# A two-part block on one core: other queues and engines for the first loads, and PSUM tiles by column part at the end

## The chip, the core and the metric

The kernel runs on one core of a Trainium2 chip. A core has TensorE (matmul, with its weight loads), VectorE, ScalarE, GpSimd and SyncE, each with its own instruction stream; the matmul sums go to PSUM, everything else lives in SBUF, and transfers between SBUF and the chip's main memory are issued by an engine's queue (here SyncE's, called SP below, and ScalarE's) and carried out by 16 DMA engines. The metric is the device time of one execution in microseconds (us). Before the change it is 1164.75 us, the median of three runs from 1164.68 to 1164.84.

## What is computed

All in float32, for 2048 tokens of 576 numbers:

```python
x = A_x
xn = _layernorm(x, axis=-1)
return x + _A_ref(xn, A_wqkv, A_wo) + _B_ref(xn, B_w1, B_w2)
```

`_A_ref` is an attention of 32 heads of 18 numbers over a dilated window: each token looks at itself and at the seven tokens 2, 4, ... 14 places before it; the result goes through `wo`. `_B_ref` is a two-layer network with a hidden width of 4608, `relu(xn @ w1) @ w2`. Both take the same normalised input and are added to `x`.

## The kernel before

**Precision.** TensorE multiplies in a faster format with fewer bits (float32r). Each operand is therefore split into a high part, the value rounded to that format, and a low part, the rest; a product takes three matmul terms (high by high, high by low, low by high). `two` (lines 144 to 150) splits a loaded weight: ScalarE copies the high part, then VectorE, or GpSimd for the steps in `by_pool`, subtracts it from the source. The normalised tokens are split in the same way when they come out of the transpose (`transpose_split`, lines 276 to 308): ScalarE writes the high part of `xT`, VectorE the low part.

**Tiling.** The tokens are dealt to two phases (`ph`) of eight tiles (`i`) of 128 tokens; pairs of tiles make four blocks of 256 tokens (`tb`). The hidden width is cut into 36 strips of 128, in 12 groups of three (`c`, `f`). One slot is one (phase, group, block, strip): `h_mm` makes 14 matmuls of 256 columns into a `ph` tile in PSUM, ScalarE and VectorE write the relu's high and low parts, and two slots later `o_mm` multiplies them by `w2`. `o_mm` handles the block's two token tiles `k` = 0 and 1, and cuts the 576 output columns in two parts `CUT`, 0 to 256 and 256 to 576, since one matmul's result must lie in one PSUM bank. Both parts of a `k` share one tile `po` of the pool `ps_o`, which has two such tiles of two banks; `half` (line 572) picks the part. After three strips `o_out` adds the sum to the accumulator, which is the tile of `x` itself. 288 slots make the whole; the attention's work is put between them by the tables `todo` and `todo_late`, and the order of all instructions is written out (`manual_schedule`).

**The opening** (lines 680 to 757) is written by hand. Line 102 sets TensorE to 24 transposes of the identity. Then the code issues the loads of `x` 0 and `x` 1 (each in two column halves, one on SP's queue and one on ScalarE's, lines 233 to 237), an Exp of one spare column on ScalarE, whose table is loaded ahead of it, the first strip of `w1`, `x` 2, three more weight strips, `x` 3, and so on. A strip of `w1` is a staging tile `st` of 640 columns: 512 rows of `w1` as four column groups, and the last 64 rows twice, in the upper and the lower partitions of the fifth (lines 157 to 162), three transfers on SP. The statistics of `x` 0 (`stats`: `bn_stats` by VectorE for each half, `bn_aggr`, an addition, two small operations by GpSimd) are followed by its normalisation on ScalarE (lines 269 and 270); those of `x` 1 by its normalisation on VectorE (line 272). TensorE transposes both (lines 286 and 287). For `x` 0 the four full groups go to one tile of `ps_m` and the rest to another; for `x` 1 both go to one tile of `ps_o`. `run_splits(-9)` on line 695 stands between the transposes of `x` 0 and its high part: it is the split of the first `w1` strip, whose step is `HEADW[0]`, -9. The first real matmuls (line 701) need its high part and the high parts of both token tiles.

**The end.** The last slot (`end` in `o_mm`) sorts its matmuls so that within each `k` the part 256 to 576 comes first, then the part 0 to 256. `o_out` (lines 611 to 617) then adds, for `k` = 0 and 1, part 1 and part 0, and issues each part's output behind its add: part 1 on ScalarE's queue, part 0 on SP's, but the very last part in two halves of 64 partitions, one on each queue. For all earlier groups one add of 576 columns (line 606) is followed, in the last group of a phase, by `done` (line 527), which issues the whole tile's output on SP when it has been called twice for the tile. `left` counts these calls.

Of the kernel before, what the change touches and what calls it, by code (L numbers as in the profile page):

```python
# [10 lines left out]
F32 = mybir.dt.float32  # L11
F32R = mybir.dt.float32r
AF = mybir.ActivationFunctionType
# [4 lines left out]
P = 128  # L18
NPH = 2
NI = 8  # L20
# [5 lines left out]
C = 3  # L26
# [12 lines left out]
HEADW = (-9, -8, -7, -6, -5, -4)  # L39
# [16 lines left out]
def tile_body(ctx: ExitStack, tc: tile.TileContext, x, wqkv, wo, w1, w2, out):  # L56
    nc = tc.nc
    S, D = x.shape
# [5 lines left out]
    KT = 4  # L64
    DR = D - KT * P
    D2 = D // 2
    CUT = (slice(0, 256), slice(256, D))
# [22 lines left out]
    ps_o = pool("ps_o", 2, space=PSUM)  # L90
    ps_h = pool("ps_h", 2, space=PSUM)
    ps_m = pool("ps_m", 2, space=PSUM)
# [10 lines left out]
    for _ in range(WARM):  # L103
        nc.tensor.transpose(warm[:, 0, 0:P], ident, ident)

    x_v = x.rearrange("(p i two) d -> two i p d", i=NI, two=NPH)
    o_v = out.rearrange("(p i two) d -> two i p d", i=NI, two=NPH)


    t = {"pe": 0.0, "dve": 0.0}  # L110

    def mm(o, l, r, start, stop, n):
        nc.tensor.matmul(o, l, r, start=start, stop=stop)  # L113
        t["pe"] += n / 2400.0 + 0.002

    def dve(n):
        t["dve"] += (n + 130) / 960.0
# [6 lines left out]
    def split_task(step, load, split):  # L124
        tasks.append((step, load, split))

    def stage_more(ahead=AHEAD):
        while tasks and len(staged) < ahead:
            step, load, split = tasks.popleft()
            st = stp.tile([P, 640], F32, name="st")  # L130
            load(st)
            staged.append((step, split, st))
# [9 lines left out]
    step_now = None  # L142

    def two(hi, lo, src, n):
        nc.scalar.activation(hi, src, AF.Copy)  # L145
        if step_now in by_pool:
            nc.gpsimd.tensor_tensor(lo, src, f32(hi), op=ALU.subtract)
        else:
            nc.vector.tensor_tensor(lo, src, f32(hi), op=ALU.subtract)  # L149
            dve(n)  # L150
# [3 lines left out]
    def w1_task(step, key, f):  # L154
        def load(st):
            c = slice(f * P, (f + 1) * P)
            nc.sync.dma_start(
                st[:, 0:512].rearrange("p (k c) -> p k c", k=KT),
                w1[0 : KT * P, c].rearrange("(k p) c -> p k c", p=P),
            )  # L160
            nc.sync.dma_start(st[0:DR, 512:640], w1[KT * P : D, c])
            nc.sync.dma_start(st[DR:P, 512:640], w1[KT * P : D, c])

        def split(st):
            w = w1p.tile([P, 2, 5 * P], F32R, name="w1t")
            two(w[:, 0, :], w[:, 1, :], st[:, :], 640)
            W1[key] = w

        split_task(step, load, split)
# [59 lines left out]
    X, XT, XN, MR = {}, {}, {}, {}  # L229

    def load_x(ph, i):
        X[ph, i] = xp.tile([P, D], F32, name="x")
        if ph == 0 and i < 2:
            for h, q in enumerate((nc.sync, nc.scalar)):
                c = slice(h * D2, (h + 1) * D2)
                q.dma_start(X[ph, i][:, c], x_v[ph, i][:, c])
            return
        nc.sync.dma_start(X[ph, i], x_v[ph, i])

    def stats(ph, i, parts=False, act=False):  # L240
        xt = X[ph, i]
# [283 lines left out]
    left = {(ph, i): 2 for ph in range(NPH) for i in range(NI)}  # L525

    def done(ph, i):
        left[ph, i] -= 1
        if left[ph, i] == 0:
            nc.sync.dma_start(o_v[ph, i], X[ph, i])  # L530


    slots = [(ph, c, tb, f) for ph in range(NPH) for c in range(NCH) for tb in range(NTB) for f in range(C)]
    H, PO = {}, {}
# [35 lines left out]
        h_out(n)  # L570

    def half(po, h):
        return po[:, 1, 0 : D - 256] if h else po[:, 0, 256:512]

    def o_mm(n, out=True, which=range(2)):
        ph, c, tb, f = slots[n]
        hi, lo = H[n]
        w = W2[ph, c, f]
        end = n == len(slots) - 1
        for k in which:  # L580
            if f == 0:
                PO[k] = ps_o.tile([P, 2, 512], F32, name="po")
            cs = slice(k * P, (k + 1) * P)
            terms = [(j, l, b, h) for j, (l, b) in enumerate(((hi, 0), (hi, 1), (lo, 0))) for h in range(2)]
            if end:
                terms.sort(key=lambda z: -z[3])
            for j, l, b, h in terms:
                mm(
                    half(PO[k], h), l[:, cs], w[:, b, CUT[h]],
                    f == 0 and j == 0, f == C - 1 and j == 2, D2,  # L590
                )
        if 1 in which:
            H.pop(n)
        if out:
            o_out(n, which)

    def o_out(n, which=range(2)):
        ph, c, tb, f = slots[n]
        if f < C - 1:
            return  # L600
        for k in which:
            i = 2 * tb + k
            acc = X[ph, i]
            if n < len(slots) - 1:
                whole = PO[k].rearrange("p b c -> p (b c)")[:, 256 : 256 + D]
                nc.vector.tensor_tensor(acc, whole, acc, op=ALU.add)  # L606
                dve(D)
                if c == NCH - 1:
                    done(ph, i)
                continue  # L610
            for h, c in reversed(list(enumerate(CUT))):
                nc.vector.tensor_tensor(acc[:, c], half(PO[k], h), acc[:, c], op=ALU.add)  # L612
                if h == 0 and i == NI - 1:
                    for q, p in (nc.sync, slice(0, P // 2)), (nc.scalar, slice(P // 2, P)):
                        q.dma_start(o_v[ph, i][p, c], acc[p, c])
                else:
                    (nc.scalar if h else nc.sync).dma_start(o_v[ph, i][:, c], acc[:, c])
            left[ph, i] -= 1
            assert left[ph, i] == 0


    todo = {}
# [10 lines left out]
    for ph in range(NPH):  # L633
# [22 lines left out]
        if ph + 1 < NPH:  # L656
            e = b + SPP - SPC
            for i in range(NI):
                if i >= len(XT_STEPS):
                    z = e + 3 + 2 * i  # L660
                    at(z - 6, load_x, ph + 1, i)
                    late(z - 2, stats, ph + 1, i)
                    late(z - 1, norm, ph + 1, i)
                    at(z + 1, make_xt, ph + 1, i)
                    continue
                load, first, second, send, back, parts = (e + k for k in XT_STEPS[i])
                at(load, load_x, ph + 1, i)
                late(first, stats, ph + 1, i, False, True)
                late(second, norm_turned, ph + 1, i)
                late(send, xt_a, ph + 1, i)  # L670
                at(back, xt_f, ph + 1, i)
                at(parts, xt_s, ph + 1, i)
# [7 lines left out]
    by_pool.update((-9, -8, *range(UNIT0 - 5, UNIT0)))  # L680
    both, x_low, w_low, last = TERMS[0:4], TERMS[4:8], TERMS[9:13], [TERMS[8], TERMS[13]]
    load_x(0, 0)
    load_x(0, 1)
    nc.scalar.activation(spare, mhalf, AF.Exp)
    stage_more(1)
    load_x(0, 2)
    stage_more(4)
    load_x(0, 3)
# [40 lines left out]
    x2[1]()  # L729
    x2[3]()  # L730
    o_mm(0)
    o_mm(1)
    make_xt(0, 3, bank=ps_h)
    o_mm(2, out=False)
    stats(0, 4)
    s5 = stats(0, 5, parts=True)
# [6 lines left out]
    h4[0]()  # L743
    h4[1]()
    o_out(2, (0,))
    x4 = make_xt(0, 4, parts=True)
    for f in x4[:3]:
        f()
    norm(0, 5)
    o_out(2, (1,))  # L750
    x4[3]()
    h_terms(5, TERMS)
# [51 lines left out]
```

## Time and profile before

| | us |
|---|---|
| median of three runs | 1164.75 (1164.68 to 1164.84) |
| the profiled execution, its own time | 1165.02 |
| its span in the profile | 1163.2 |
| TensorE matmul busy in the span | 1155.8 (99%) |
| VectorE busy | 822.1 (71%) |
| ScalarE busy | 308.7 (27%) |
| GpSimd busy | 44.8 (4%) |

The span is the part of the execution that the profiler's records cover. Times in the rows below are counted from its start. In a row of the timeline stand the start, the length, the engine, the line of the kernel, the operation, output and inputs by the program's names with their shapes (partitions by columns), and how many instructions were merged; what ended an idle time before it stands in brackets. PE is TensorE, DVE VectorE, ACT ScalarE, POOL GpSimd, and SPq and ACTq are the queues of SyncE and ScalarE while they issue transfers. A row of the waits has the engine and what it waited for, then the total in us, how often, and the longest. A row of DMA issues has the transfer, the queue, how often and its size, and the median us from issue to landing. A row of windows has a stretch of time and its length, the busy time and the number of instructions of the five engines (PE, weight loads, DVE, ACT, POOL), the clock granted to TensorE, the busy share of the DMA engines and the GB/s that they moved.

### The profile page before, as it was taken

To read this page: it belongs to the slowest core of one execution; us is meant where nothing else is said; L and a number is where in the kernel's file an instruction comes from. 1 tells how busy PE (TensorE), PEld (TensorE's weight loads), DVE (VectorE), ACT (ScalarE), POOL (GpSimd) and SP (SyncE) were. 2 spreads that over 40 slices of the span, in tenths; PEclk is the share of its full clock that TensorE was granted. 3 is DMA by queue.
4 is the path that set the end of the run, shared out by engine and by line. 5 is a ranking of instruction groups with operands and counts; after the bars stand their busy time and mean duration, and the time that the engine had idled before them with its cause. 6 is when DMAs were issued, how large, how long until landed. Compare 5 with 4: busy or idle time off the path is not lost.

```text
span 1163.2 us, 21702 instructions
## 1 busy us (share of the span) xinstructions
PE 1155.8 (99%) x8916; PEld 1147.9 (99%) x8916; DVE 822.1 (71%) x1299; ACT 308.7 (27%) x748; POOL 44.8 (4%) x60
## 2 busy tenths in 40 slices
PE   8999999999999999999999999999999999999998
PEld 8999999999999999999999999999999999999998
DVE  7427885887687688876683288768768877887843
ACT  5312222131231221322433123222222312222310
POOL 3200100010000000000010001000100000000000
PEclk9999999999999999999999999999999999999999
DMA  5312211140331311364752113031312303113541
GB/s 184 98 34 77 70 47 54 39 112 1 94 81 30 89 34 44 96 163 106 184 159 70 42 53 96 21 81 40 85 36 59 110 1 101 50 31 91 125 99 62
DMA packets 150036, 88.66 MB, mean 76 GB/s; under 512 B 58560, under 2 KB 133824, under 8 KB 149936
## 3 DMA queue, kind: packets, MB, share of 16 engines
q1 hardware_dynamic: 146752, 78.38, 25.1%
q10 hardware_dynamic: 3184, 8.88, 2.6%
q8 instruction: 70, 1.15, 0.4%
q14 instruction: 30, 0.25, 0.1%
HBM read 67.90 MB, written 11.14 MB: 68 GB/s over the span
## 4 chain that ended last, share of the span: by engine, by line
PE 99%; DMA 0%; ACT 0%; DVE 0%; issue 0%; DVEq 0%; POOL 0%; ACTq 0%
PE ph L113 39%; PE po L113 39%; PE pm L113 20%; PE pm L286 0%; DMA x<-in_x 0%; DVE x L612 0%; PE pm L287 0%; DVE bst L250 0%; ACT xn L269 0%; ACT xn L270 0%; ACT xT L291 0%; PE po L286 0%; DVEq L800 0%; PE ph L287 0%; POOL nm L256 0%
## 5 line engine op out<-in xcount | busy, mean ns | idle before, releaser
L113 PE MATMUL ph<-xT,w1t 128*128 128x256 f32 x4018 | 505.1, 277 | 0.7 <-ACT xT L291 0.7
L113 PEld LDWEIGHTS ph<-xT,w1t 128*128 128x128 f32 x4018 | 487.0, 188 | 1.3 <-ACT xT L291 1.0
L113 PE MATMUL po<-w2t,hhi 128*128 128x256 f32 (+1 forms) x2304 | 395.3, 293 | 0.0
L113 PEld LDWEIGHTS po<-w2t,hhi 128*128 128x128 f32 x2304 | 337.3, 188 | 1.1
L556 ACT ACTIVATE hhi<-ph 128x256 fp32r<-128x256 f32 x287 | 109.9, 383 | 582.9 <-PE ph L113 570.5
L113 PE MATMUL po<-w2t,hlo 128*128 128x256 f32 (+1 forms) x1152 | 243.9, 292 | 0.0
L559 DVE SCALAR_TENSOR_TENSOR hlo<-ph,hhi 128x256 fp32r<-128x256 f32 x287 | 120.7, 421 | 165.0 <-ACT hhi L556 164.4
L113 PEld LDWEIGHTS po<-w2t,hlo 128*128 128x128 f32 x1152 | 190.1, 187 | 0.0
L113 PE MATMUL pm<-wq,xT 128*128 128x432 f32 x896 | 185.5, 358 | 0.0
L606 DVE TENSOR_TENSOR x<-po,x 128x576 f32<-128x576 f32 x190 | 143.0, 756 | 60.1 <-PE po L113 57.3
L113 PEld LDWEIGHTS pm<-wq,xT 128*128 128x128 f32 x896 | 163.8, 188 | 5.6
L421 DVE TENSOR_TENSOR pr<-qo,k 128x1152 f32<-128x1152 f32 x64 | 86.1, 1348 | 0.0
L424 DVE TENSOR_REDUCE lg<-pr 128x64 f32<-128x1152 f32 x64 | 85.1, 1343 | 0.0
L451 DVE TENSOR_TENSOR pr<-lg,v 128x1152 f32<-128x1152 f32 x64 | 84.7, 1349 | 0.0
L149 DVE TENSOR_TENSOR w2t<-st,w2t 128x576 fp32r<-128x576 f32 x72 | 55.8, 775 | 31.4 <-ACT w2t L145 31.4
L149 DVE TENSOR_TENSOR w1t<-st,w1t 128x640 fp32r<-128x640 f32 x70 | 58.8, 840 | 20.6 <-ACT w1t L145 20.5
L458 DVE TENSOR_TENSOR pr<-pr 128x288 f32<-128x288 f32 (+1 forms) x128 | 70.5, 600 | 0.0
L145 ACT ACTIVATE w2t<-st 128x576 fp32r<-128x576 f32 x72 | 49.3, 685 | 44.0 <-PE po L113 34.5
L390 ACT ACTIVATE k<-pm 128x144 f32<-128x144 f32 x64 | 18.7, 292 | 146.2 <-PE pm L113 146.2
L145 ACT ACTIVATE w1t<-st 128x640 fp32r<-128x640 f32 x72 | 52.8, 734 | 12.7 <-DMA st<-in_w 6.7
L427 POOL TENSOR_SCALAR_AFFINE_SELECT lg<-lg 1x512 f32<-1x512 f32 x8 | 9.9, 1232 | 810.0 <-DVE lg L424 810.0
L522 DVE TENSOR_TENSOR x<-pm,x 128x256 f32<-128x256 f32 (+1 forms) x32 | 13.1, 453 | 30.8 <-PE pm L113 30.8
(79 smaller groups left out, 461.8 us busy)
## 6 DMA issues: line engine op xcount, KB each, us to landing
st<-in_w SPq DMA_DIRECT2D x72, 288.0 KB, 3.2
st<-in_w SPq DMA_DIRECT2D x72, 256.0 KB, 3.2
st<-in_wqkv SPq DMA_DIRECT2D x32, 216.0 KB, 3.0
turned<-tr SPq DMA_DIRECT2D x64, 80.0 KB, 2.8
xn<-turned SPq DMA_DIRECT2D x16, 320.0 KB, 3.2
st<-in_w SPq DMA_DIRECT2D x144, 32.0 KB, 2.8
x<-in_x SPq DMA_DIRECT2D x14, 288.0 KB, 4.1
out<-x SPq DMA_DIRECT2D x14, 288.0 KB, 2.1
```

Source lines behind the costliest of these rows:

```text
L113: nc.tensor.matmul(o, l, r, start=start, stop=stop)
L145: nc.scalar.activation(hi, src, AF.Copy)
L149: nc.vector.tensor_tensor(lo, src, f32(hi), op=ALU.subtract)
L390: nc.scalar.activation(k[:, W - 1 + i, :], pq[:, 1, :], AF.Copy)
L421: nc.vector.tensor_tensor(pr[i], q, window(k, i), op=ALU.mult)
L424: nc.vector.tensor_reduce(lg[:, i], pr.pop(i).rearrange(heads, d=Dh), axis=AX.X, op=ALU.add)
L451: nc.vector.tensor_tensor(pr[i].rearrange(heads, d=Dh), e, window(v, i).rearrange(heads, d=Dh), op=ALU.mult)
L458: nc.vector.tensor_tensor(o, z[:, 0:n], z[:, n : 2 * n], op=ALU.add)
L522: nc.vector.tensor_tensor(acc, po[h], acc, op=ALU.add)
L556: nc.scalar.activation(hi, pt, AF.Relu)
L559: nc.vector.scalar_tensor_tensor(lo, pt, 0.0, f32(hi), op0=ALU.max, op1=ALU.subtract)
L606: nc.vector.tensor_tensor(acc, whole, acc, op=ALU.add)
```

## The change

There are three edits.

- **The first loads.** Both halves of `x` 0 go on SP's queue. `x` 1 is one transfer of all its columns on ScalarE's queue. It is issued from within the load of the first `w1` strip, whose two 64-row transfers also go on ScalarE's queue, one ahead of `x` 1 and one behind it. `stage_more(1)` therefore moves ahead of the spare Exp.
- **The first high part.** For the step `HEADW[0]`, which is the first `w1` strip alone, VectorE copies the high part.
- **The last two token tiles.** In the last group of three slots, `k` = 0 takes both tiles of `ps_o`, one for each part of the columns, and `k` = 1 takes two tiles of `ps_m`. `x` 6 of the second phase goes out whole by `done` after both adds; the two parts of `x` 7 go out by one transfer each.

```diff
     def two(hi, lo, src, n):
-        nc.scalar.activation(hi, src, AF.Copy)
+        if step_now == HEADW[0]:
+            nc.vector.tensor_copy(hi, src)
+        else:
+            nc.scalar.activation(hi, src, AF.Copy)
...
+            if key == (0, 0, 0):
+                nc.scalar.dma_start(st[0:DR, 512:640], w1[KT * P : D, c])
+                load_x(0, 1)
+                nc.scalar.dma_start(st[DR:P, 512:640], w1[KT * P : D, c])
+                return
             nc.sync.dma_start(st[0:DR, 512:640], w1[KT * P : D, c])
             nc.sync.dma_start(st[DR:P, 512:640], w1[KT * P : D, c])
...
     def load_x(ph, i):
         X[ph, i] = xp.tile([P, D], F32, name="x")
-        if ph == 0 and i < 2:
-            for h, q in enumerate((nc.sync, nc.scalar)):
-                c = slice(h * D2, (h + 1) * D2)
-                q.dma_start(X[ph, i][:, c], x_v[ph, i][:, c])
+        if ph == i == 0:
+            for c in slice(0, D2), slice(D2, D):
+                nc.sync.dma_start(X[ph, i][:, c], x_v[ph, i][:, c])
             return
-        nc.sync.dma_start(X[ph, i], x_v[ph, i])
+        (nc.scalar if (ph, i) == (0, 1) else nc.sync).dma_start(X[ph, i], x_v[ph, i])
...
     def half(po, h):
+        if isinstance(po, list):
+            return po[h]
         return po[:, 1, 0 : D - 256] if h else po[:, 0, 256:512]
...
-            if f == 0:
+            if f == 0 and n == len(slots) - C:
+                if k:
+                    PO[k] = [ps_m.tile([P, c.stop - c.start], F32, name="pm") for c in CUT]
+                else:
+                    PO[k] = [ps_o.tile([P, 2, 512], F32, name="po")[:, 0, 0 : c.stop - c.start] for c in CUT]
+            elif f == 0:
                 PO[k] = ps_o.tile([P, 2, 512], F32, name="po")
...
             for h, c in reversed(list(enumerate(CUT))):
                 nc.vector.tensor_tensor(acc[:, c], half(PO[k], h), acc[:, c], op=ALU.add)
-                if h == 0 and i == NI - 1:
-                    for q, p in (nc.sync, slice(0, P // 2)), (nc.scalar, slice(P // 2, P)):
-                        q.dma_start(o_v[ph, i][p, c], acc[p, c])
-                else:
+                if k:
                     (nc.scalar if h else nc.sync).dma_start(o_v[ph, i][:, c], acc[:, c])
-            left[ph, i] -= 1
-            assert left[ph, i] == 0
+            if k == 0:
+                done(ph, i)
...
     load_x(0, 0)
-    load_x(0, 1)
+    stage_more(1)
     nc.scalar.activation(spare, mhalf, AF.Exp)
-    stage_more(1)
     load_x(0, 2)
```

## The prediction

> **What bounds the kernel now.** I read the head of the page first, then the waits of TensorE over the whole span, then the chain of work that ended last in the opening, and at last the timeline, the DMA issues and the windows at the two places that the change touches.
>
> ```profile
> span 1163.2 us, 21702 instructions
> ...
> PE 1155.8 (99%) x8916; PEld 1147.9 (99%) x8916; DVE 822.1 (71%) x1299; ACT 308.7 (27%) x748; POOL 44.8 (4%) x60
> ```
>
> ```profile
> PE po L104 <- POOL mhalf L99: 1.4, 1, 1.4
> PE pm L286 <- ACT xn L270: 1.2, 1, 1.2
> PE ph L113 <- ACT xT L291: 0.7, 1, 0.7
> ```
>
> These three are all the waits that the profile lists for TensorE: 3.3 us, all in the first 8.84 us. Span less busy is 1163.2 - 1155.8 = 7.4 us; the other 4.1 us lie behind the last matmul. From 8.84 us to that matmul TensorE never waits for anything, so a change in the opening moves everything behind it by the same amount, and a change at the end counts by itself. No part of the change alters the number of matmuls or the order between. Whatever it is worth lies in the first 9 and the last 5 us.
>
> The opening, from the chain of waits (start, length, what):
>
> ```profile
> 0.73 2.92 DMA x<-in_x
> ...
> 3.67 0.83 DVE bst L250 x2
> ...
> 5.08 0.79 ACT xn L269
> ...
> 6.78 0.66 PE pm L286 x4
> ...
> 8.19 0.61 ACT xT L291
> ...
> 8.84 3.74 PE ph L113 x28
> ```
>
> The path to the first real matmul begins with the landing of the first half of x 0 at 3.65 us; statistics (L250, two halves, ending 4.50), normalisation on ScalarE, transposes on TensorE and the copy of x 1's transposes to xT follow with gaps of hundredths. Anything that delays the statistics of x 0 delays the whole kernel.
>
> The end, from the timeline:
>
> ```profile
> 1157.57 0.31 PE L113 MATMUL po<-w2t,hlo 128*128 128x320 f32 x1
> ...
> 1157.95 0.28 PE L113 MATMUL po<-w2t,hlo 128*128 128x256 f32 x1
> ...
> 1158.27 1.60 DVE L612 TENSOR_TENSOR x<-po,x 128x320 f32<-128x320 f32 x4 [3.07 <-PE po L113]
> 1158.36 0.31 PE L113 MATMUL po<-w2t,hlo 128*128 128x320 f32 x1
> ...
> 1158.74 0.28 PE L113 MATMUL po<-w2t,hlo 128*128 128x256 f32 x1
> 1158.80 1.13 ACTq L617 DMA_DIRECT2D out<-x  x2
> ...
> 1159.90 0.52 SPq L615 DMA_DIRECT2D out<-x  x1
> 1160.02 0.55 ACTq L615 DMA_DIRECT2D out<-x  x1
> ```
>
> The sums of the four parts are complete at 1157.88 (x 6, 320 columns), 1158.23 (x 6, 256), 1158.67 (x 7, 320) and 1159.02 (x 7, 256). VectorE begins its first add at 1158.27, 0.04 behind the second of these, though that add needs the first alone. From there the four adds run back to back, to 1159.87. So VectorE is late by 1158.27 - 1157.92 = 0.35 us, and this delay reaches the last output transfer.
>
> **The change part by part: the opening.**
>
> ```profile
> 0.73 0.90 ACTq L236 DMA_DIRECT2D x<-in_x  x2
> 0.73 0.87 SPq L236 DMA_DIRECT2D x<-in_x  x2
> ...
> 1.66 1.28 ACT L684 ACT_TABLE_LOAD   x1 [1.66 <-PEq L786]
> 2.12 0.56 SPq L161 DMA_DIRECT2D st<-in_w  x1
> ...
> 4.84 0.81 DVE L250 BATCH_NORM_STATS2 bst<-x 128x6 f32<-128x288 f32 x2
> ...
> 6.63 0.72 ACT L145 ACTIVATE w1t<-st 128x640 fp32r<-128x640 f32 x1
> 6.75 0.58 DVE L272 TENSOR_SCALAR xn<-x,mv,rstd 128x576 f32<-128x576 f32 x1 [0.67 <-POOL rstd L257]
> ...
> 7.27 0.27 PE L287 MATMUL pm<-ident,xn 128*64 128x128 f32 x1
> ...
> 7.43 1.55 POOL L147 TENSOR_TENSOR w1t<-st,w1t 128x640 fp32r<-128x640 f32 x1 [0.72 <-ACT w1t L145]
> 7.47 0.60 ACT L291 ACTIVATE xT<-pm 128x512 fp32r<-128x512 f32 x1
> ...
> 7.88 0.27 PE L287 MATMUL po<-ident,xn 128*64 128x128 f32 x1
> ...
> 8.10 0.69 DVE L294 TENSOR_TENSOR xT<-pm,xT 128x512 fp32r<-128x512 f32 x1 [0.77 <-ACT xT L291]
> ```
>
> Median microseconds from issue to landing, from the DMA issues of narrow windows (the first two issued at 0.73, the third at about 1.15, the w1 transfer at 1.65):
>
> ```profile
> x<-in_x ACTq DMA_DIRECT2D x1, 144.0 KB, 3.1
> x<-in_x SPq DMA_DIRECT2D x1, 144.0 KB, 2.9
> ...
> x<-in_x SPq DMA_DIRECT2D x1, 144.0 KB, 3.2
> ...
> st<-in_w SPq DMA_DIRECT2D x1, 256.0 KB, 4.0
> ```
>
> *The second half of x 0* moves from ScalarE's queue (issued 0.73, landed 3.83) to second place on SP (issue at 0.73 + 0.41 = 1.14, half of the 0.87 for two). Today that place holds the first half of x 1, which lands 3.2 us after issue. The second statistics instruction starts today at about 4.08 (3.67 and half of 0.83), so its data has 0.25 us of slack now and loses it. Ends: with the 2.9 us of the quickest row it lands at 4.04, and nothing is lost; if the first half lands sooner because less is issued beside it, some 0.1 is won. With the 4.0 us of the w1 row it lands at 5.14, a loss of 1.1. With the nearest row, 3.2, at 4.34, and the instruction starts at 4.36: a loss of 0.3. Beside it ScalarE's queue now carries 32 KB and then 288 KB of x 1, where it had two times 144 KB, so up to that time somewhat less competes, and I take 4.25: **+0.2 us**. The Trainium skill (DMA: Bandwidth & Descriptors, "Issuing engines are not separate DMA queues") says that issuing from several engines saves nothing but issue time. By that rule the half comes 0.41 later than today, at 4.24, which gives +0.2 as well, and it speaks against the step.
>
> *x 1 on ScalarE's queue* is issued behind one 0.56 us issue of w1, at about 1.29. Landing after 3.2 to 4.0 us it is there at 4.5 to 5.3; VectorE wants it at 4.84, shifted to 5.04. If it is 0.25 late, only the normalisation of x 1 is late, which ends at 7.33 while TensorE is at x 0's transposes until 7.54: 0.2 of cover. Cost 0, at worst 0.05 beyond the +0.2.
>
> *ScalarE* issues three transfers (0.56, about 0.43 and 0.56) ahead of its table load, which moves from 1.66 to about 2.3 and, with the 0.2 us spare Exp behind it, ends by 3.9. Its next work is the normalisation at 5.08: hidden, with 1.2 to spare. *SP* issues the two w1 remainders no longer, so all behind them, x 2 first, is issued 1.1 us earlier; TensorE waits for no transfer after 8.84, so that is worth 0 for the time. The w1 part itself is issued on SP at the same place, and lands about 5.65; its remainders come earlier than today.
>
> *The w1 high part on VectorE.* ScalarE loses 0.72 us at 6.63 to 7.35, but its next instruction (7.47) waits for TensorE's transposes to 7.44: gain 0. VectorE takes it up behind L272 at 7.33. The nearest row is L272 itself, one source, 0.58 for 576 columns, so 0.64 for 640, ending at 7.97; the low part's two-source form would give 0.84, ending 8.17. VectorE's next work is the low part of xT at 8.10, so the cost is 0, at most 0.07. GpSimd's w1 low part starts at 8.0 in place of 7.43 and ends at 9.6 instead of 8.98; its readers are the last 10 of the 28 matmuls that start at 8.84, the first of them some 16 x 0.134 = 2.1 us in, at 11: hidden. If GpSimd were 1.4 us later still, TensorE would wait here.
>
> **The end.** With a PSUM tile per part, each add waits for its own three matmuls. That a tile decides what is waited for is in the opening rows: x 0's transposes lie in two tiles, and ScalarE starts at 7.47, before the last of them (L287) ends at 7.54; x 1's lie in one, and ScalarE starts at 8.19, behind L287's end at 8.15. The adds then start at 7.92, 8.33, 8.74 and 9.15 (1158.27 + 1.60 = 1159.87, at 0.41 a step) and the last ends at 1159.53: 0.34 earlier. The last transfer changes too: one of 128 KB on SP in place of two of 64 KB, of which ScalarE's is the later.
>
> ```profile
> out<-x ACTq DMA_DIRECT2D x1, 160.0 KB, 1.9
> out<-x SPq DMA_DIRECT2D x1, 128.0 KB, 1.9
> ...
> out<-x ACTq DMA_DIRECT2D x1, 64.0 KB, 2.2
> ```
>
> ```profile
> 1160.00:1160.50 0.50, 0.00 (x0) 0.00 (x0) 0.00 (x0) 0.00 (x0) 0.00 (x0) 1.00 1.03 344
> ...
> 1161.00:1161.50 0.50, 0.00 (x0) 0.00 (x0) 0.00 (x0) 0.00 (x0) 0.00 (x0) 0.86 0.79 191
> ```
>
> Today the last lands at 1160.02 + 2.2 = 1162.2. Afterwards: x 6 whole, issued on SP at 1158.77 when both its adds are done; 160 KB of x 7 on ScalarE's queue at 1159.25; 128 KB on SP at 1159.56. By the 1.9 of such a transfer the last lands at 1161.46, 0.75 sooner. But the first bytes start no earlier than today (issue 1158.77 against 1158.80), and 576 KB (590,000 bytes) at the 344 GB/s of the window row take 1.7 us, so the last may be held by those before it. Ends: -0.75 and, if only the adds' gain counts, -0.34. I take **-0.55 us**.
>
> The sum: +0.2 + 0 + 0 - 0.55 = -0.35 us. The profiled execution took 1165.02 us (span 1163.2), 0.27 above the median of the three runs, 1164.75. So 1164.67 for a profiled execution and 1164.4 for the median.
>
> **The rivals.**
>
> *B, the transfers are served in order of issue.* The x halves in the rows above landed at 3.65, 3.83 and 4.35, in the order of their issue. After the change only the first half and 32 KB of w1 stand ahead of x 0's second half, so it would land at 4.04 or before; the statistics then end up to 0.1 sooner than now. Against it: the later issue is certain, and 288 KB start 0.15 us behind. Sum -0.1 - 0.55 = -0.65: 1164.1. The Trainium skill (DMA: Bandwidth & Descriptors, "Queues, rings and completion order") has each engine change queues only after a whole packet of many descriptors, which would favour this order; the trace, with three landings in order, doesn't contradict it.
>
> *C, x 0's second half lands late.* x 1's rows are now one piece of 2304 bytes where they were two of 1152; if each queue gets turns by row, x 1 takes two thirds of the rate and x 0's second half ends with it, near the w1 row: 4.0 us, +1.1. With the end's -0.55 that is +0.55: 1165.3, slower than before. It decides from a landing of 4.05 + 0.55 = 4.6 on. For it: some 0.6 MB are asked for within half a microsecond. Against: the same place served 144 KB in 3.2 us against equal traffic. A worse form exists: TensorE's idle stretch before 6.78 is 1.2 us now; at the end, TensorE stops at 1159.02 and its clock is 0.86 on the mean of 1161.0 to 1161.5, so it falls 2.0 to 2.5 us after the last matmul. A stretch that long in the opening would put some of the first matmuls at half clock, 2 to 3 us.
>
> *D, the separate tiles change no wait* (the adds were held by something else). Then adds as today; the last transfer is issued at 1159.9 and lands 1.9 later, 1161.8: -0.4 at best, -0.1 if the stream holds it. With +0.2: 1164.7.
>
> **How the numbers follow.** Forecast 0.5, B 0.23, C 0.15, D 0.12. The likeliest gives 1164.4, with its own range 1163.9 to 1164.8. The range for eight in ten reaches to B's lower end (1164.75 - 0.2 - 0.75 = 1163.8) and into C's milder half: 1163.7 to 1165.1. What a measurement here can tell from no change is about 0.2%, 2.3 us, and no case but C's worse form gets that far: same 0.95, slower 0.03; faster 0.02 for what I have not seen.
>
> **What would show it.** In the changed profile: x 0's halves land 0.4 to 0.7 us apart, the second statistics instruction shows a wait for x of its own, and the first matmul of `ph` starts at 9.0 (8.7 under B, 9.9 under C). The first L612 add starts at 1157.9 of today's count, 0.35 before x 6's last matmul ends, and the four adds show a wait for TensorE each. The last output transfer lands 2.4 to 2.6 us after the last matmul's end (3.2 now). VectorE's copy of w1 takes 0.64 and ends before L294's start. The forecast is wrong if a TensorE wait appears after the first `ph` matmul, or if `xT` waits for VectorE's copy.

## The result and the profile after

The changed kernel takes 1166.87 us, the median of 21 executions; the kernel before takes 1164.68 us beside them (21 executions, 1164.50 to 1165.19). The ratio is 1.0017, with a 95% interval of 1.0010 to 1.0023: slower, by 2.2 us where 0.35 us faster was forecast, and outside the range of 1163.7 to 1165.1.

The median hides the shape. The 21 executions run from 1164.89 to 1168.60, and each comes with the mean clock that TensorE was granted:

| mean clock | executions | times, us | median, us | above before |
|---|---|---|---|---|
| 0.999 or 1.000 | 8 | 1164.89 to 1165.74 | 1165.26 | 0.6 |
| 0.997 or 0.998 | 13 | 1166.50 to 1168.60 | 1167.39 | 2.7 |

Nothing lies between 1165.74 and 1166.50. So there are two losses to explain: one that all executions have, and one of about 2.1 us that 13 of 21 have on top. The profiled execution (1165.58 us, span 1163.8) belongs to the first group, and shows the first loss alone; no execution of the second group was profiled for this kernel. Its page begins:

```profile
span 1163.8 us, 21695 instructions
...
PE 1155.9 (99%) x8916; PEld 1147.9 (99%) x8916; DVE 822.9 (71%) x1300; ACT 308.1 (26%) x747; POOL 44.9 (4%) x60
```

TensorE is as busy as before, 1155.9 us to 1155.8, in a span that is 0.6 longer: what was lost is idle time. (Line numbers are 7 to 14 higher than before: L250 is now L257, L272 L279, L286 L293, L294 L301, L612 L626.) The waits of TensorE over the whole span (total us, times, longest):

```profile
PE po L293 <- DVE xn L279: 1.8, 1, 1.8
PE po L104 <- POOL mhalf L99: 1.4, 1, 1.4
PE ph L113 <- ACT xT L298: 0.7, 1, 0.7
PE pm L293 <- ACT xn L277: 0.3, 1, 0.3
```

A new wait heads the list. The transposes of `x` 1 (L293 into `po`) wait 1.8 us for `x` 1's normalised tokens; the wait for those of `x` 0 has shrunk from 1.2 to 0.3. The chain that ended last, in the opening:

```profile
1.18 2.33 DMA x<-in_x
...
3.53 0.47 DVE bst L257
...
7.62 0.57 POOL rstd L264
...
8.21 0.59 DVE xn L279
...
8.85 0.66 PE po L293 x4
...
10.29 3.73 PE ph L113 x28
```

The first real matmul starts at 10.29, 1.45 us behind the 8.84 of before. The transfer at the head of this chain is `x` 0's second half, and the chain names no other: it goes on through GpSimd, where 2.43 us up to 7.58 are put down to "issue". The timeline says which transfer GpSimd had to wait for, by way of VectorE:

```profile
1.36 0.59 ACTq L245 DMA_DIRECT2D x<-in_x  x1
...
2.12 0.51 SPq L245 DMA_DIRECT2D x<-in_x  x1
...
2.98 1.02 DVE L257 BATCH_NORM_STATS2 bst<-x 128x6 f32<-128x288 f32 x2 [2.98 <-DMA x<-in_x]
...
6.28 0.66 PE L293 MATMUL pm<-ident,xn 128*128 128x128 f32 x4 [0.35 <-ACT xn L277]
6.28 0.82 DVE L257 BATCH_NORM_STATS2 bst<-x 128x6 f32<-128x288 f32 x2 [1.86 <-DMA x<-in_x]
...
7.62 0.56 POOL L264 TENSOR_TENSOR rstd<-mv,mhalf 128x1 f32<-128x1 f32 x1 [2.47 <-DVE mv L261]
...
8.71 0.49 DVE L146 CAST w1t<-st 128x640 fp32r<-128x640 f32 x1
```

and the DMA issues of narrow windows have the landings:

```profile
x<-in_x SPq DMA_DIRECT2D x1, 144.0 KB, 2.2
...
x<-in_x SPq DMA_DIRECT2D x1, 144.0 KB, 2.3
...
x<-in_x ACTq DMA_DIRECT2D x1, 288.0 KB, 4.9
...
st<-in_w SPq DMA_DIRECT2D x1, 256.0 KB, 5.4
```

`x` 0 is there sooner than before, both halves (2.2 and 2.3 us after issue, where the first two took 2.9 and 3.1): its statistics start at 2.98 instead of 3.67 and its transposes at 6.28 instead of 6.78. `x` 1 is issued at 1.36, takes 4.9 us and lands at 6.26, where its halves landed at 4.35 and about 4.6. VectorE is through with `x` 0 at 4.4 and sits idle for 1.86 us. Everything of `x` 1 is late by about that, and TensorE with it.

The end, in the timeline:

```profile
1159.01 0.82 DVE L626 TENSOR_TENSOR x<-po,x 128x320 f32<-128x320 f32 x2 [2.72 <-PE po L113]
...
1159.83 0.28 PE L113 MATMUL pm<-w2t,hlo 128*128 128x256 f32 x1
...
1160.65 0.33 SPq L628 DMA_DIRECT2D out<-x  x1
```

The adds no longer begin behind `x` 6's last matmul, and the last transfer is issued 0.54 us behind the last matmul's end (1160.11), where it was 1.00 (1160.02 to 1159.02).

### The profile page after: what moved, and what is told of

Read it like the earlier page. It is cut to its first block, busy times and chain, and to the rows that moved or that the text cites. A ratio compares the mean times of both kernels' runs of the same rounds, so it can differ in the third digit from the quotient of the medians.

```text
span 1163.8 us, 21695 instructions
## 1 busy us (share of the span) xinstructions
PE 1155.9 (99%) x8916; PEld 1147.9 (99%) x8916; DVE 822.9 (71%) x1300; ACT 308.1 (26%) x747; POOL 44.9 (4%) x60
## 4 chain that ended last, share of the span: by engine, by line
PE 99%; issue 0%; DVE 0%; DMA 0%; POOL 0%; ACT 0%; SPq 0%; DVEq 0%; POOLq 0%
PE ph L113 39%; PE po L113 38%; PE pm L113 20%; PE pm L293 0%; DMA x<-in_x 0%; DVE x L626 0%; POOL rstd L264 0%; PE pm L294 0%; PE po L293 0%; ACT xT L298 0%; DVE xn L279 0%; DVE bst L257 0%; SPq L243 0%; DVEq L810 0%; PE ph L294 0%
## 5 line engine op out<-in xcount | busy, mean ns | idle before, releaser
L113 PE MATMUL po<-w2t,hhi 128*128 128x256 f32 x2292 | 393.0, 293 | 0.0
L113 PE MATMUL po<-w2t,hlo 128*128 128x256 f32 x1146 | 242.4, 292 | 0.0
```

## The experiments

One table for all. "Wait for x 1" is TensorE's wait for the normalised tokens of `x` 1 in the profiled execution, "ph" the start of the first real matmul there, the last column the executions with a mean clock of 0.998 or less. The experiments were run in three groups, each with the kernel before beside it, which had none of these (33, 29 and 33 executions; medians 1164.86, 1164.69 and 1164.72).

| kernel | median (range), us | wait for x 1 | ph | clock 0.998 or less |
|---|---|---|---|---|
| changed kernel | 1166.87 (1164.89 to 1168.60) | 1.8 | 10.29 | 13 of 21 |
| end alone | 1164.44 (1164.17 to 1164.63) | none | 8.89 | 0 of 11 |
| opening alone | 1167.59 (1166.12 to 1169.27) | 1.6 | 10.11 | 9 of 11 |
| x 1 on SP | 1165.02 (1164.62 to 1165.29) | 1.0 | 9.88 | 0 of 11 |
| 10 fillers | 1165.82 (1165.42 to 1167.95) | 0.6 | 10.15 | 1 of 11 |
| 15 fillers | 1165.44 (1165.13 to 1166.37) | none | 10.10 | 0 of 11 |
| x 1 in halves | 1168.00 (1165.79 to 1168.72) | 2.0 | 10.65 | 8 of 9 |
| before, x 1 whole | 1165.17 (1164.98 to 1165.41) | none | 9.22 | 0 of 11 |
| x 1 first | 1165.07 (1164.56 to 1167.22) | none | 9.65 | 2 of 11 |
| x 1 later | 1168.38 (1167.39 to 1169.11) | 3.1 | 12.18 | 8 of 8 |
| SP held | 1164.65 (1164.34 to 1165.04) | 0.5 | 9.03 | 0 of 11 |
| end and w1 copy | 1164.24 (1164.07 to 1164.50) | none | 8.81 | 0 of 11 |
| end, halves in order | 1164.69 (1164.27 to 1165.13) | none | 8.56 | 0 of 11 |

### Which part costs: the end alone, and the opening alone

The first is the kernel before with the third edit only; the second is the changed kernel with the end of before.

```diff
-            if f == 0:
+            if f == 0 and n == len(slots) - C:
+                if k:
+                    PO[k] = [ps_m.tile([P, c.stop - c.start], F32, name="pm") for c in CUT]
+                else:
+                    PO[k] = [ps_o.tile([P, 2, 512], F32, name="po")[:, 0, 0 : c.stop - c.start] for c in CUT]
+            elif f == 0:
                 PO[k] = ps_o.tile([P, 2, 512], F32, name="po")
...
```

> The kernel before with the edit of the end alone. Theory (the opening alone costs, the end gains): the last transfer lands 2.4 to 2.6 us after the last matmul instead of 3.2, so 1164.68 - 0.6 = about 1164.1 us, all executions within 0.5 us of each other, clock 0.999 to 1.000. Rival (the separate tiles at the end disturb something, and with it the spread): 1166 to 1167 with executions several us apart.

> The changed kernel with the end of before. Theory: the changed kernel's median and the end's gain back, 1166.9 + 0.6 = about 1167.5 us, executions spread over 3 to 4 us, x 1 lands near 6.3 and the first ph matmul starts 1 us or more behind 8.84. Rival (the end brings the spread): 1166.1 us, 1.45 above before, within 0.5 us of each other.

The end alone: 1164.44 us beside 1164.86 (ratio 0.9996, 0.9987 to 1.0004), 0.42 won, and steady, though 0.3 above the 1164.1 expected. The opening alone: 1167.59 (ratio 1.0024, 1.0015 to 1.0033), with the spread, as the theory had it. The interval of the end alone takes in 1; that it gains is shown by its timeline more than by its time. The rival that the new tiles disturb something has fallen. The timeline of the end, in the kernel with the end alone:

```profile
1157.92 0.82 DVE L619 TENSOR_TENSOR x<-po,x 128x320 f32<-128x320 f32 x2 [2.72 <-PE po L113]
...
1158.71 0.82 DVE L619 TENSOR_TENSOR x<-pm,x 128x320 f32<-128x320 f32 x2
1158.77 0.33 SPq L530 DMA_DIRECT2D out<-x  x1
...
1159.23 0.37 ACTq L621 DMA_DIRECT2D out<-x  x1
...
1159.56 0.33 SPq L621 DMA_DIRECT2D out<-x  x1
```

The first add starts 0.35 us sooner than the 1158.27 of before, ahead of the end of `x` 6's last matmul, and the transfers are issued at 1158.77, 1159.23 and 1159.56. Each lands 2.1 us after its issue, so the last at 1161.66, where it was 1162.2: 0.54 sooner, with the last matmul ending at 1159.02 in both.

### What slows 13 of 21 executions: fillers, and a longer wait

Transposes of the identity, as the kernel has them at its start, were put between the transposes of `x` 0 and `x` 1, ten and then fifteen; and in another kernel `x` 1 was issued behind the second remainder of `w1`, in the code behind the spare Exp.

```diff
     x0 = make_xt(0, 0, parts=True)
+    for _ in range(FILL):
+        nc.tensor.transpose(warm[:, 0, 0:P], ident, ident)
```

```diff
                 nc.scalar.dma_start(st[0:DR, 512:640], w1[KT * P : D, c])
-                load_x(0, 1)
                 nc.scalar.dma_start(st[DR:P, 512:640], w1[KT * P : D, c])
...
     nc.scalar.activation(spare, mhalf, AF.Exp)
+    load_x(0, 1)
```

> The changed kernel with ten more transposes of the identity between the transposes of x 0 and those of x 1, so that TensorE isn't idle while it waits for x 1. Theory (in the longer executions TensorE's clock falls behind the long idle stretch): x 1 and the first ph matmul are as late as in the changed kernel (about 10.3), but the clock is 0.999 to 1.000 in all executions and the time 1164.9 to 1165.9, without the ones above 1166.5. Rival (the longer executions are those in which x 1 lands later still, and the clock follows the idle time only): spread as in the changed kernel, 1164.9 to 1168.6.

> The changed kernel with fifteen transposes of the identity (ten before) between those of x 0 and x 1. Theory (the clock falls behind TensorE's idle stretch): the stretch is nearly closed, every execution has a clock of 0.999 or more, and the times lie between 1165.2 and 1166.2 us. Rival (something else slows the longer executions): again one or more in ten at 0.998 and above 1167 us.

> The changed kernel, but x 1 is issued behind the table load and the spare Exp on ScalarE, about 2.5 us later, to make TensorE's idle stretch longer on purpose. Theory (a long idle stretch lowers TensorE's clock): the idle stretch is 3 to 4 us, the windows behind it show a clock of 0.5 for 2 to 4 us, every execution has a mean clock of 0.998 or lower, and the time is 2 to 3 us above what the later start alone gives (about 1167.5): 1169.5 to 1170.5 us. Rival (the clock has no part in it): clock 1.00 in all windows and 1167 to 1168 us.

Ten fillers left 0.6 us of the wait, and one execution of eleven (1167.95, clock 0.998) was still slowed. Fifteen closed it: all eleven at 0.999 or more, none above 1166.37, with the first real matmul nearly as late as in the changed kernel (10.10). Only the idleness of TensorE in the wait for `x` 1 was taken away, and the second loss went with it. The later `x` 1 did the opposite: all eight executions at 0.998 or 0.997. (It was issued at 2.06, 0.7 later and not 2.5, and the time is 1168.38, below the 1169.5 to 1170.5 expected.) Its windows behind the wait, the clock third from the end:

```profile
8.00:9.00 1.00, 0.00 (x0) 0.00 (x0) 0.79 (x4) 0.00 (x0) 0.06 (x1) 1.00 0.84 169
9.00:10.00 1.00, 0.00 (x0) 0.00 (x0) 0.47 (x1) 0.00 (x0) 0.49 (x1) 0.77 0.91 319
...
14.00:16.00 2.00, 2.00 (x12) 2.00 (x11) 1.81 (x5) 0.00 (x0) 0.90 (x2) 0.50 1.14 358
16.00:18.00 2.00, 2.00 (x17) 2.00 (x17) 0.48 (x2) 1.05 (x3) 0.00 (x0) 0.91 0.87 287
```

A mean of 0.77 over a microsecond that ends at 0.50 puts the fall at 9.54, and 0.91 over the two from 16 puts the return at 16.36: 6.8 us at half clock, longer than the 2 to 4 expected. TensorE had finished `x` 0's transposes at 7.05, so the clock fell 2.5 us behind that.

The clock's own records in the traces are sharper, and suggest why the clock falls in some executions of a kernel only. In every profile the first record of a full clock begins at another time, from 4.24 to 7.01 us. Where the clock doesn't fall, it stays full for 338, 339 or 340 times 3.413 us, until behind the last matmul. In the two slowed profiles (this one, and that of `x` 1 in halves, below) it is full for 3.41 us, half for 6.83, which is twice that, and full again for 337 times as long. So the clock changes only at the ends of stretches of 3.41 us, and these begin at another point of the program in each execution. The five profiles with the most idleness of TensorE in one such stretch:

| profile | stretch, us | TensorE idle in it, us | clock behind it |
|---|---|---|---|
| x 1 later | 6.14 to 9.55 | 2.5 | half |
| x 1 in halves | 6.33 to 9.74 | 2.0 | half |
| opening alone | 5.00 to 8.41 | 1.7 | full |
| changed kernel | 4.97 to 8.38 | 1.7 | full |
| x 1 first | 5.84 to 9.25 | 1.5 | full |

By these five the limit lies between 1.7 and 2.0 us of idleness in one stretch. In the changed kernel's profile the boundary at 8.38 cuts the wait of 1.8 us (7.05 to 8.85) in two. That the slowed executions of this kernel are those in which the boundary lies elsewhere is inferred, since none of them was profiled. The slowed executions of two other kernels stay unexplained: one of eleven with ten fillers, where the profile has waits of 0.6 and 0.7, and two of eleven of `x` 1 first, where it has 1.2 (for `x` 0) and 0.7, the same two waits as the kernel before, which fell in none of 95.

### Why x 1 is late: three ways to issue it

One transfer of whole rows on SP, behind `x` 0 and ahead of `w1`; two transfers of half rows at the same place of ScalarE's queue; the whole at the head of ScalarE's queue.

```diff
                 nc.scalar.dma_start(st[0:DR, 512:640], w1[KT * P : D, c])
-                load_x(0, 1)
                 nc.scalar.dma_start(st[DR:P, 512:640], w1[KT * P : D, c])
...
-        (nc.scalar if (ph, i) == (0, 1) else nc.sync).dma_start(X[ph, i], x_v[ph, i])
+        nc.sync.dma_start(X[ph, i], x_v[ph, i])
...
     load_x(0, 0)
+    load_x(0, 1)
     stage_more(1)
```

```diff
-        if ph == i == 0:
+        if ph == 0 and i < 2:
             for c in slice(0, D2), slice(D2, D):
-                nc.sync.dma_start(X[ph, i][:, c], x_v[ph, i][:, c])
+                (nc.scalar if i else nc.sync).dma_start(X[ph, i][:, c], x_v[ph, i][:, c])
```

```diff
+                load_x(0, 1)
                 nc.scalar.dma_start(st[0:DR, 512:640], w1[KT * P : D, c])
-                load_x(0, 1)
                 nc.scalar.dma_start(st[DR:P, 512:640], w1[KT * P : D, c])
```

> The changed kernel with x 1 as one transfer on SP, behind both halves of x 0 and ahead of w1; the two w1 remainders stay on ScalarE's queue. Theory (x 1 is late because w1 and x 2 on SP share the DMA engines with it): x 1 lands by 5.0, the first ph matmul starts at 8.5 to 9.0, 1163.8 to 1164.4 us, spread under 0.5 us. Rival (a whole tile in one transfer of 2304-byte rows is slow by itself, wherever it is issued): x 1 lands near 6.0, the ph matmul at 10, 1166 us or more, and spread.

> The changed kernel, but x 1 in two transfers of half its columns, both still on ScalarE's queue between the two w1 remainders. Theory W (rows of 2304 bytes start with a hole in the DMA stream, so x 1 as whole rows is late by itself): no hole near 3.3 us, x 1 lands by 4.9, the first ph matmul at 8.4 to 8.9, 1163.8 to 1164.4 us, all within 0.6. Theory S (w1 and x 2, asked for on SP at the same time, take the rate): x 1 lands near 6, ph at about 10, 1165 to 1168 us as the changed kernel.

> The changed kernel, but x 1 goes first on ScalarE's queue, ahead of both w1 remainders (issue 0.73 in place of 1.36). If only its place in the queue makes x 1 late, it lands 0.6 earlier, at about 5.6, the ph matmul moves to 9.7 and TensorE's idle stretch between the transposes shrinks to about 1.2: 1164.8 to 1165.3 us without executions above 1166.5. If it also pushes x 0 back (its rows then compete from the start), x 0 lands 0.3 to 0.7 later and less is won.

None was clean. On SP, `x` 1 was issued at 1.65 and landed 4.2 us later, at 5.85: sooner than 6.26 though issued later, but not by 5.0 as the theory wanted. The landing and the first real matmul (9.88) came near the rival's 6.0 and 10; the time, 1165.02 and steady, did not come near its 1166 or more. In halves it landed later still, at 6.06 and 6.9, so rows of 2304 bytes alone are not the cause, and theory W fell. First in its queue it landed 3.6 us after issue, at 4.33, but `x` 0 on SP then took 3.4 and 3.6 and landed at 4.1 and 4.8: the loss moved to `x` 0. The median, 1165.07, was as expected, but two of eleven executions were slowed where none was expected. The kernel with halves was profiled in a slowed execution; its windows show the same fall, 2.6 us behind the end of `x` 0's transposes (7.14), while its wait of 2.0 us was already over at 9.16:

```profile
9.00:10.00 1.00, 0.81 (x5) 0.50 (x5) 1.00 (x3) 0.00 (x0) 0.42 (x1) 0.87 0.63 115
...
14.00:16.00 2.00, 2.00 (x12) 2.00 (x11) 0.34 (x1) 0.25 (x1) 0.00 (x0) 0.50 0.80 242
16.00:18.00 2.00, 2.00 (x17) 2.00 (x17) 1.69 (x4) 1.66 (x4) 0.00 (x0) 0.86 1.01 357
```

From 9.74 to 16.56, again 6.8 us.

### Why x 1 is late: whole in the kernel before, and SP held back

In the kernel before, `x` 1 whole on ScalarE's queue behind `x` 0's second half; and in the changed kernel, SP made to wait with `w1` and all behind it until `x` 0's first half is there. (The column that VectorE copies is overwritten by the `w1` transfer.)

```diff
-        if ph == 0 and i < 2:
+        if (ph, i) == (0, 1):
+            nc.scalar.dma_start(X[ph, i], x_v[ph, i])
+            return
+        if ph == i == 0:
```

```diff
             c = slice(f * P, (f + 1) * P)
+            if key == (0, 0, 0):
+                nc.vector.tensor_copy(st[:, 0:1], X[0, 0][:, 0:1])
             nc.sync.dma_start(
```

> The kernel before, but x 1 as one transfer of all columns on ScalarE's queue, behind x 0's second half; nothing else. Theory W: x 1 lands at 5.5 to 6, the statistics of x 1 wait about 1 us, ph at 9.6 to 10, 1165.6 us or more. Theory S: w1 starts 0.4 earlier on SP and competes as well, so x 1 is late here too, by less: 5.0 to 5.5, ph at 9.2, about 1165.2 us.

> The changed kernel, but SP waits with the first w1 strip, and so with all behind it, until x 0's first half has landed (VectorE copies one column of it into the staging tile first, which the w1 transfer overwrites). x 1 then has the DMA engines nearly to itself from its issue at 1.36 until about 4.1. Theory S (w1 and x 2 on SP take the rate): x 1 lands at 4.3 to 4.7 instead of 6.26 and its statistics no longer wait long; w1 lands near 7, the ph matmul at 8.7 to 9.2, 1164.0 to 1164.6 us without executions above 1165.5. Rival (the late landing comes with x 1's own place and time in the stream): x 1 lands at 5.5 or later, ph at 9.5 or later, 1165 us and more.

Whole in the kernel before, it took 4.0 us and landed at 5.18; ph at 9.22, 1165.17 us: theory S's numbers. With SP held, it took 3.7 us instead of 4.9 from the same issue time, 1.35, and landed at 5.05; its statistics waited 0.56 us, ph came at 9.03, and the time fell from 1166.87 to 1164.65, steady, beside 1164.72 for the kernel before. The timeline:

```profile
1.35 0.60 ACTq L247 DMA_DIRECT2D x<-in_x  x1
...
3.07 0.15 DVE L161 COPY st<-x 128x1 f32<-128x1 f32 x1 [3.07 <-DMA x<-in_x]
...
3.25 0.39 SPq L162 DMA_DIRECT2D st<-in_w  x1
...
5.03 0.82 DVE L259 BATCH_NORM_STATS2 bst<-x 128x6 f32<-128x288 f32 x2 [0.56 <-DMA x<-in_x]
```

So what SP asks for at the same time costs `x` 1 1.2 us of its landing, most of its delay, and with that both losses against the kernel before. It is not all: 4.3 to 4.7 was expected, and 5.05 came; with the gain of the end in it, this kernel should be 0.4 below the kernel before, and is level with it.

No run holds back `x` 2 or `w1` alone, but the trace of the changed kernel has every packet with its queue and size. `x` 1's 128 rows (2304 bytes) begin from 2.88 to 5.68. In that time 422 packets of `w1` (512 bytes each, 512 to a strip) begin on SP, from 3.27 on, and 42 of `x` 2's 128 rows, none before 4.95. So it is `w1` above all that runs beside `x` 1. In the kernel before, `x` 1's rows begin up to 4.08, and `w1`'s first packet only at 3.70: half of `x` 1 stood ahead of `w1` in the same queue.

### The copy of w1 by VectorE, and all halves in order

```diff
-        nc.scalar.activation(hi, src, AF.Copy)
+        if step_now == HEADW[0]:
+            nc.vector.tensor_copy(hi, src)
+        else:
+            nc.scalar.activation(hi, src, AF.Copy)
```

```diff
-            for h, q in enumerate((nc.sync, nc.scalar)):
-                c = slice(h * D2, (h + 1) * D2)
-                q.dma_start(X[ph, i][:, c], x_v[ph, i][:, c])
+            for c in slice(0, D2), slice(D2, D):
+                nc.sync.dma_start(X[ph, i][:, c], x_v[ph, i][:, c])
```

> The edit of the end, and of the opening only the first w1 high part on VectorE, with the loads of before. If this part is worth nothing, as the prediction had it: 1164.4 us, as the end alone, within 0.15; the copy takes 0.49 and ends before the low part of xT starts at 8.1; GpSimd's low parts come later and nobody waits. If it costs: the first ph matmul stays at 8.84 and one of the 28 behind it waits, +0.1 to +0.3.

> The edit of the end, and all four halves of x 0 and x 1 on SP in this order, with the w1 strip whole behind them on SP as before; nothing on ScalarE's queue. Theory (what lands first is what has least beside it): x 0's halves land at about 3.0 and 3.5, x 1's at 4.1 and 4.7; x 0's statistics end at 4.0, those of x 1 at 5.2, the ph matmul starts at 8.4: 1164.0 us, steady. Rival (rows that stall near 3 to 4 us hit x 1 here too): x 1 lands at 5 or later, ph at 9, 1164.6 us or more.

The end with the copy gives 1164.24 us beside 1164.72 (ratio 0.9996, 0.9987 to 1.0005): 0.48 won where the end alone won 0.42, so the copy is worth nothing that shows. This is the quickest kernel of the study: it keeps the loads of before, its median lies below both kernels', and its executions reach from 1164.07 to 1164.50 where the kernel before beside it has 1164.44 to 1165.19, though the interval of the ratio takes in 1.

All halves in order on SP brings the first real matmul to 8.56, the earliest of all and close to the theory's 8.4, with `x` 1's statistics at 4.51 behind no wait for it. It is no quicker all the same, 1164.69 where the theory had 1164.0: SP issues 0.9 us later for everything behind, and a second wait of TensorE appears further on:

```profile
PE po L113 <- DVE w2t L149: 0.3, 1, 0.3
```

From the first real matmul to the end of the last (1159.43) this kernel needs 1150.87 us, 0.69 more than the kernel before; the 0.3 of the wait are part of that, and the rest stays open.

## Why the prediction was wrong

**The step that failed** is the one on `x` 1: "Landing after 3.2 to 4.0 us it is there at 4.5 to 5.3 ... Cost 0, at worst 0.05 beyond the +0.2." It landed 4.9 us after issue, at 6.26, beyond the upper bound, and cost 1.45 us at the first real matmul. The bound was taken from rows in which `x` 1's first half stood ahead of `w1` in one queue; none of them had 288 KB on one queue beside 256 and then 288 KB on the other.

**What made it fail** was taken for free: "The w1 part itself is issued on SP at the same place", and "all behind them, x 2 first, is issued 1.1 us earlier; TensorE waits for no transfer after 8.84, so that is worth 0". The place was the same, but `x` 1 no longer stood ahead of `w1` there, and `w1` ran beside it; `x` 2, issued at 2.12 instead of 3.36, joined for the last part. Holding both back took 1.2 us off the landing and 2.2 us off the median.

**x 0's second half**: "+0.2 us" was wrong in sign. It landed 2.3 us after issue instead of the 3.2 of the nearest row, at 3.51, with `x` 1 no longer beside it from the start (with `x` 1 first in its queue, `x` 0 took 3.4 and 3.6), and `x` 0's transposes came 0.5 us sooner. Rival B had seen that direction, and gave it up to 0.1 us. By the sentence from the Trainium skill (DMA: Bandwidth & Descriptors, "Issuing engines are not separate DMA queues") the half would come later by its issue time; here what ran beside it weighed more than the 0.41 us of issue.

**The worse form of C** came true with `x` 1 in the place of `x` 0. It was given 0.03 with "2 to 3 us" as its price. The price was right: 2.1 us between the two groups. The threshold was not. It was read off the end of the trace, where TensorE stops for good (2.0 to 2.5 us until the fall), as the length that one stretch of idleness must have. Here the kernels with a wait of 1.6 to 2.0 us fell in 30 of 41 executions, the one with 1.0 in none of 11, and in the kernel with halves the clock fell 0.6 us after TensorE had resumed: by the clock records, what counts is the idleness within stretches of 3.41 us that begin at times of their own, 2.0 us of it in a profile where the clock fell, 1.7 in two where it did not. The Trainium skill (TensorE: Matmul & The Clock Gate, "Part 1: The HAM clock gate") has the clock judged over free-running windows of about 3.4 us, and lowered after an idle one. The clock records agree with the windows; they do not agree that a whole window must be idle.

**The copy of w1**: cost 0, right, with 0.49 us instead of 0.64 (L146 above). In the changed kernel it is no test, since all is late there; in the kernel with the loads of before it is one, and TensorE shows no wait for it.

**The end**: right in mechanism and size. The four adds and the issues at 1158.77, about 1159.25 and 1159.56 came within 0.03 in the kernel with the end alone. The last transfer landed 0.54 sooner where -0.55 was forecast, between the two ends given for it: the transfers took 2.1 us, not 1.9, so it landed at 1161.66 and not 1161.46. The medians differ by 0.42, and what makes up the 0.1 is not shown. Rival D has fallen.

The sum as measured, from the two profiles: +1.45 at the first real matmul, less 0.36 that TensorE made up between the first real matmul and the last (1150.18 us before, from 8.84 to 1159.02; 1149.82 after, from 10.29 to 1160.11), less 0.54 at the end, gives +0.55. The profiled executions differ by 0.56 (1165.58 and 1165.02), and the executions with a full clock by 0.6. Why TensorE made up that time, and in some kernels with a late start and not in that of the opening alone, stays open. The other 2.1 us of 13 executions are the clock.

## What to carry to other kernels

A load that nobody waits for yet still has a price: ask what stands ahead of and beside each load that somebody does wait for, and try holding the rest back. Judge a stall early in a kernel not by its length alone; TensorE's clock may fall behind it, and then a further loss comes on top (2.1 us here behind a wait of 1.8), in some executions and not in others, so the times of all executions and their clocks are to be read, not one profile. Independent edits at the two ends of a kernel should be measured apart: here the end won about 0.5 us by its timeline, which the opening hid.

## What was not expected of the hardware

The stream of transfers thins out just where `x` 1 is awaited. In the changed kernel's windows the rate falls from 293 GB/s to 117, two fifths, with `x` 1, the first `w1` strip and `x` 2 all asked for:

```profile
2.00:3.00 1.00, 1.00 (x7) 1.00 (x6) 0.02 (x1) 0.48 (x1) 0.00 (x0) 1.00 0.95 293
3.00:3.50 0.50, 0.50 (x4) 0.50 (x3) 0.44 (x1) 0.50 (x1) 0.00 (x0) 1.00 1.30 159
3.50:4.00 0.50, 0.50 (x5) 0.50 (x4) 0.46 (x1) 0.49 (x2) 0.00 (x0) 1.00 0.43 117
```

The share of 0.43 does not mean that the engines were free. A packet is counted where it begins, and those that began from 3.0 to 3.5, with a share above 1, ran on past 3.5: of `x` 1's 128 rows 20 took over 0.2 us and up to 1.2, most of them begun between 2.9 and 3.8, where a row of this size takes 0.093 us elsewhere. With SP held, nearly alone, `x` 1 still took 3.7 us and had 18 such rows, up to 0.74 us. So it isn't the rate alone that the transfers share. In the kernel with `x` 1 in halves the same half microsecond, from 3.5 to 4.0, has 182 GB/s and a share of 0.65 where 2 to 3 had 291 and 0.93, so the length of the rows isn't it alone either; and `x` 1 whole in the kernel before had no row over 0.1 us. What these rows wait for stays open.

A transfer's time to landing also depended on what was issued beside it more than on its size: 32 KB took from 2.4 to 5.8 us in these kernels, 144 KB from 2.2 to 5.0, and 288 KB from 3.6 to 5.9.
